# Top-k attention with a low-rank mixer: masking by a widened difference in the first two batches, and other rounding of the parameters

## The chip, the core and the metric

The kernel runs on one core of one Trainium2 chip. The metric is the device time of one execution in microseconds (us), the median over repeated runs. The core's engines work side by side, each through its own queue in program order: TensorE (PE, with its weight loads shown apart as PEld), VectorE (DVE), ScalarE (ACT), GpSimd (POOL) and SyncE (SP), which issues the transfers.

## What is computed

Eight batches, eight heads, 576 positions, head width 64. Attention keeps in each row of scores the 32 largest; its result is mixed along the sequence by two thin matrices of rank 32, and goes through a two-layer network with a residual.

```python
scores = scale * np.matmul(q, k.transpose(0, 1, 3, 2))
kth = np.partition(scores, -top_k, axis=-1)[..., -top_k:-top_k + 1]
mask = scores >= kth
scores = np.where(mask, scores, -1000000000.0)
scores = scores - np.max(scores, axis=-1, keepdims=True)
attn = np.exp(scores)
attn = attn / (np.sum(attn, axis=-1, keepdims=True) + 1e-09)
x = np.matmul(attn, v)                    # heads side by side: (batch, seq, 512)
h = x.transpose(0, 2, 1) @ U @ V          # rank 32
u = x + h.transpose(0, 2, 1)
out = u + np.maximum(u @ w_ch1, 0.0) @ w_ch2
```

The four parameters `U`, `V`, `w_ch1`, `w_ch2` arrive as 64-bit floating-point numbers. The engines have no such type, so the kernel takes the two 32-bit words of each number apart and joins them to a 32-bit number with integer and floating-point operations.

## The kernel before

**Steps.** Two heads form a pair `g`; a batch has four pairs, so `g` runs from 0 to 31. A pair has five blocks of query rows: `t` = 0 to 3 with 128 rows, in which the two heads are two chunks of scores side by side, and `t` = 4 with the last 64 rows of both heads, stacked into one chunk. A step is `n = 5 g + t`, and the loop over `n` (L561) writes out by hand in which order the parts of neighbouring steps go into the engines' queues. Batch 0 is `n` = 0 to 19; `ALONE` is 20.

**The parts of a step.** `scores(g, t)` multiplies on PE and lets ACT copy the scores to `Ssb`, which has three buffers. `front(g, t)` is a generator: each `yield` hands back to the loop, which decides when its next part is issued. It finds the 32nd largest score of each row on DVE in four rounds of "the eight largest" (`first` L317, then `m` L329) with three replacements between them (`rr` L325). Then it masks and weighs. Head 0 (chunk 0) was weighed early by ACT (`weigh`, the Exp of L297, right after `nmax` L321), and DVE masks its weights with L334, which also gives their sum. Head 1 is masked by POOL: L332 writes a large negative number where a score is under the threshold, L333 adds it to the scores, and ACT weighs after that, with the sum from the accumulator. The weights are `E`, with three buffers. `turns(g, t)` turns `E` on PE in pieces of four, four and one transposes (two pieces for `t` = 4), and ACT copies each piece to `PT`. `values(g, t)` multiplies `PT` by the values; ACT copies the product to `XT`, or for `t` = 4 scales it into `x` with the reciprocal of the sums `den` (L377 adds 1e-9, L378 inverts).

**Mixer and network.** `mixed(g, wait)` turns `XT` back, scales it on POOL (L419), multiplies by `U` (`pT`, `Tb`) and `V` and adds the residual (`up`), which gives `uT`, the input of the network. `mlp(b)` yields after every matmul: L462 for the first layer, whose result ACT passes through Relu to `hT` (L474), and L481 for the second. `fill()` takes from it a share of matmuls at fixed places of a step, so that batch b's network runs among the attention steps of batch b+1. In batch 0 there is no network to fill with.

**Parameters.** `next_params` moves 36 slabs through three stages: a load from memory (`f64_raw`), `f64_parts` with three ACT operations (L157, L159, L160) and a maximum on POOL (L158), and in the next call `f64_join` with a shift on DVE (L168) and two additions on POOL (L169, L171).

**The order in step n, up to ALONE.** First `first` of n; the rest of the turns of n-2; `scores` of n+1; `values` of n-2; `nmax` and the early Exp of n with its first round of replacements; `next_params`; the first piece of turns of n-1; the late Exp of n-1; the further rounds of n; its masks. After ALONE the same parts are spread between calls of `fill()`. PE, ACT, DVE and POOL keep the order in which the program issues.

Of the kernel before, what the change touches and what calls it, by code (L numbers as in the profile page):

```python
# [14 lines left out]
TOPK = 32  # L15
NEG = -3.0e38

TINY = 2.0**-15


@with_exitstack
def kernel(
# [80 lines left out]
    U = const.tile([P, NT + 1, R], F32, name="U")  # L103

    V = const.tile([NT * R, S], F32, name="V")

    step = const.tile([P, 1], F32, name="step")
    nc.vector.memset(step, 2.0**23)
    nudge = const.tile([P, 1], F32, name="nudge")
    nc.vector.memset(nudge, 0.4 * TINY)  # L110

    def rows(t):
        return P if t < NT else TAIL
# [27 lines left out]
    def f64_parts(raw, out):  # L141

        n, w = raw.shape[0], raw.shape[-1] // 2
        d = "p f" if len(raw.shape) == 3 else "p"
        low, hi = (raw.rearrange(f"{d} (w two) -> {d} w two", two=2)[..., i] for i in range(2))
        low8 = raw.bitcast(U8).rearrange(f"{d} (w eight) -> {d} w eight", eight=8)[..., 3]
        if out is None:
            if not spare:  # L150

                uT = mlpp.tile([P, NC, S], F32, tag="uT", name="uT")
                words = uT.rearrange("p c n -> p (c n)").bitcast(U32)
                spare.extend(words[:, i * SLAB : (i + 1) * SLAB] for i in range(NT))
            out = spare.pop()[0:n, 0:w]
        bits = out.bitcast(U32)
        nc.scalar.activation(bits.bitcast(F32), hi.bitcast(F32), AF.Abs)  # L157
        nc.gpsimd.tensor_scalar(bits.bitcast(F32), bits.bitcast(F32), TINY, None, ALU.max)  # L158
        nc.scalar.activation(low, low8, AF.Identity, bias=step[0:n], scale=(1 + 2.0**-10) / 32)  # L159
        nc.scalar.activation(hi.bitcast(F32), hi.bitcast(F32), AF.Sign, bias=nudge[0:n])  # L160
        return hi, bits, low

    def f64_join(hi, bits, low, outs):

        nc.vector.tensor_single_scalar(bits, bits, 3, ALU.logical_shift_left)  # L168
        nc.gpsimd.tensor_tensor(bits, bits, hi, ALU.add)  # L169
        for dst, form in outs:  # L170
            nc.gpsimd.tensor_tensor(dst.bitcast(U32), form(bits), form(low), ALU.add)  # L171
# [123 lines left out]
    def weigh(chunk, E, nmax, total=None):  # L295

        nc.scalar.activation(E, chunk, AF.Exp, bias=nmax, scale=SCALE, accum_out=total)  # L297

    def front(g, t):

        if t == 0:
            dens[g] = small.tile([P, 2 * NT + 1], F32, tag="den", name="den", bufs=3)
        chunks, den = S2s.pop((g, t)), dens[g]
        n = len(chunks)
        E2 = attn.tile([P, 2 * S], F32, tag="E", name="E", bufs=3)
        Es = [E2[:, c * S : (c + 1) * S] for c in range(n)]
        sums = [den[:, 2 * t + c : 2 * t + c + 1] for c in range(n)]
        probs[g, t] = E2  # L310
        curs, ms = list(chunks), [None] * n
        first = small.tile([P, 2, 8], F32, tag="first", name="first", bufs=3)
        nmax = small.tile([P, 2], F32, tag="nmax", name="nmax", bufs=4)
        order = (1, 0) if n == 2 else (0,)
        for c in order:
            ms[c] = first[:, c]
            nc.vector.max(ms[c], curs[c])  # L317
        yield
        for i in range(1, TOPK // 8):
            if i == 1:  # L320
                nc.scalar.mul(nmax[:, 0:n], first[:, 0:n, 0], -SCALE)  # L321
                weigh(chunks[0], Es[0], nmax[:, 0:1])
            for c in order:
                nxt = attn.tile([P, S], F32, tag="rr", name="rr", bufs=3)
                nc.vector.match_replace(nxt, ms[c], curs[c], NEG)  # L325
                curs[c] = nxt
            for c in order:
                ms[c] = small.tile([P, 8], F32, tag="m8", name="m8", bufs=8)
                nc.vector.max(ms[c], curs[c])  # L329
            yield  # L330
        if n == 2:
            nc.gpsimd.tensor_scalar(Es[1], chunks[1], ms[1][:, 7:8], NEG, ALU.is_lt, ALU.mult)  # L332
            nc.gpsimd.tensor_tensor(chunks[1], chunks[1], Es[1], ALU.add)  # L333
        nc.vector.scalar_tensor_tensor(  # L334
            out=Es[0],
            in0=chunks[0],
            scalar=ms[0][:, 7:8],
            in1=Es[0],
            op0=ALU.is_ge,
            op1=ALU.mult,  # L340
            accum_out=sums[0],
        )
        if t == NT:
            del qkTs[g]
        yield
        if n == 2:
            weigh(chunks[1], Es[1], nmax[:, 1:2], sums[1])
        yield

    def turns(g, t):  # L350
# [16 lines left out]
        nc.scalar.copy(PT[:, NT * nh], tp)  # L367
        yield

    def values(g, t):  # L370

        PT = PTs.pop((g, t))
# [1 line left out]
        O = ps_t.tile([P, P], F32, tag="tp", name="O")  # L374
        if t == NT:
            den, x = dens[g], xs[g % 2]
            nc.vector.tensor_scalar_add(den, den, 1e-9)  # L377
            nc.vector.reciprocal(den, den)  # L378
            for j in range(NT + 1):
                nc.tensor.matmul(  # L380
                    O,
# [23 lines left out]
    def mixed(g, wait):  # L405

        b, gi = divmod(g, NPAIR)
        if gi == 0:
            uTs[b] = mlpp.tile([P, NC, S], F32, tag="uT", name="uT")
        XT, den = XTs.pop(g), dens.pop(g)  # L410
        X = xs[g % 2]
        tp = ps_t.tile([P, NT, P], F32, tag="tp", name="tp")
        for t in range(NT):
# [141 lines left out]
    t = 0  # L555
# [5 lines left out]
    for n in range(STEPS + 2):  # L561
# [6 lines left out]
            fronts[n] = front(g, t)  # L568
            next(fronts[n])
        here, last = fronts.get(n, iter(())), fronts.pop(n - 1, iter(()))  # L570
        if n <= ALONE:
            next(turning, None)
            next(turning, None)
            if n < ALONE:
                scores(*divmod(n + 1, CH))
            fill()
            if n >= 1:
                turning = turns(*divmod(n - 1, CH))
            if n == ALONE:

                next(turning)
                next(turning)
            if n >= 2:
                values(*divmod(n - 2, CH))
            next(here)
            if n == ALONE:
                values(*divmod(n - 1, CH))
                mixing.append(mixed((n - 1) // CH, 1))
                fill()
                scores(*divmod(n + 1, CH))  # L590
                while mixing:
                    fill()
            next_params(1)
            if n and n < ALONE:
                next(turning)
            fill()
            next(last, None)
            next(ready, None)
            next(here)
            fill()  # L600
            if n >= 2 and (n - 2) % CH == NT:
                mixing.append(mixed((n - 2) // CH, 3))
            next(here)
            if n in (11, 16):
                next_params(1)
            next(here)
            fill()
            continue
        fill()
        next(turning, None)  # L610
        fill()
        next(turning, None)
        fill()
# [4 lines left out]
        if n + 1 < STEPS:  # L618
            scores(*divmod(n + 1, CH))
        next(here, None)  # L620
        next_params(1)
        if n - 2 >= ALONE and (n - 2) % CH == NT:
            mixing.append(mixed((n - 2) // CH, 4))
# [2 lines left out]
        fill()  # L626
        if n <= STEPS:
            turning = turns(*divmod(n - 1, CH))
        next(turning, None)
        fill()  # L630
        next(here, None)
        next(last, None)
# [37 lines left out]
```

## Time and profile before

| | us |
|---|---|
| median of 10 runs | 1872.44 |
| lowest and highest | 1869.05 and 1873.53 |
| the profiled execution | 1873.53 |
| its span, from the first instruction to the last | 1871.6 |
| PE busy in the span | 1754.3 (94%) |
| DVE busy | 1621.1 (87%) |
| ACT busy | 1009.5 (54%) |
| POOL busy | 689.3 (37%) |
| mean granted clock of PE | 0.963 |

The profile is one execution. In its strips the span is cut into 40 slices of some 47 us, with the busy share of each in tenths. In a timeline a row gives start, duration, engine, line, operation, what is written and read, how many instructions were merged, and in brackets how long the engine was idle before and what ended that. A row of stretches gives, for PE, PEld, DVE, ACT and POOL, the busy time in the stretch, then the granted clock of PE, the share of the transfer engines and the rate.

The groups that the change touches, from the profile's list of groups: L334 on DVE 160 times, 854 ns each, 136.7 us; L332 on POOL 128 times, 2242 ns, 287.0 us; L333 on POOL 128 times, 1409 ns, 180.3 us; L297 on ACT 288 times, 777 ns, 223.9 us.

### The profile page before, as it was taken

The page shows a single profiled execution, that of the slowest core. Times are in us where ns is not written, and L with a number is a line of the kernel's source. Part 1 is how long each engine was busy: PE and PEld are TensorE (multiplying, and loading weights), DVE is VectorE, ACT ScalarE, POOL GpSimd, SP SyncE. Part 2 cuts the span into 40 slices and gives each one's busy share as a digit, 9 for nine tenths or more (in the row PEclk, how much of TensorE's full clock was granted, in tenths as well). Part 3 has the DMA queues.
Part 4 walks back from the last instruction along what each step waited for, and adds up shares of the span by engine and source line. Part 5 has one row for each costly group of instructions (what it writes and reads, how often), then busy time and mean ns, then how long its engine had stood idle before and what let it go on. Part 6 is the DMA issues. An engine that isn't in the chain of part 4 may idle for free.

```text
span 1871.6 us, 29270 instructions
## 1 busy us (share of the span) xinstructions
PE 1754.3 (94%) x10528; PEld 1327.3 (71%) x10528; DVE 1621.1 (87%) x3312; ACT 1009.5 (54%) x2467; POOL 689.3 (37%) x470
## 2 busy tenths in 40 slices
PE   5565698999999999999999999999999999999999
PEld 3444466688677877788777877778777877778777
DVE  7999989899999999999999999999999999996000
ACT  4566676665555555555555556565655655554211
POOL 3667688533223332332323333323233232322000
PEclk7667799999999999999999999999999999999999
DMA  3222222100001010101001010010001010000000
GB/s 86 65 71 74 73 82 77 41 24 24 17 18 31 21 32 20 28 22 26 14 24 30 22 32 19 23 27 20 21 20 31 24 30 21 9 8 7 6 14 12
DMA packets 127296, 58.23 MB, mean 31 GB/s; under 512 B 89904, under 2 KB 124976, under 8 KB 127152
## 3 DMA queue, kind: packets, MB, share of 16 engines
q1 hardware_dynamic: 126096, 56.10, 11.2%
q8 instruction: 84, 1.38, 0.3%
q14 instruction: 60, 0.49, 0.1%
q10 hardware_dynamic: 1056, 0.26, 0.1%
HBM read 46.89 MB, written 9.44 MB: 30 GB/s over the span
## 4 chain that ended last, share of the span: by engine, by line
PE 82%; DVE 11%; ACT 3%; POOL 1%; issue 1%; DMA 0%; DVEq 0%; POOLq 0%; SPq 0%; ACTq 0%
PE mm L462 27%; PE mm L481 25%; PE sc L271 8%; PE O L393 6%; PE tp L361 6%; DVE rr L325 4%; DVE m L329 4%; PE up L437 2%; PE O L380 2%; DVE first L317 1%; PE O L390 1%; PE tp L251 1%; DVE E L334 1%; PE tp L509 1%; PE up L439 1%
## 5 line engine op out<-in xcount | busy, mean ns | idle before, releaser
L329 DVE MAX8 m<-rr 128x8 f32<-128x576 f32 x864 | 614.8, 749 | 5.3
L481 PE MATMUL mm<-hT,w 128*128 128x256 f32 (+1 forms) x2048 | 562.7, 410 | 0.0
L462 PE MATMUL mm<-uT,w 128*128 128x256 f32 (+1 forms) x2048 | 558.3, 411 | 1.5 <-ACT hT L474 1.5
L332 POOL TENSOR_SCALAR E<-Ssb,m 128x576 f32<-128x576 f32 x128 | 287.0, 2242 | 621.5 <-DVE m L329 498.2
L462 PEld LDWEIGHTS mm<-uT,w 128*128 128x128 f32 x2048 | 363.9, 190 | 108.5 <-issue 28.0
L481 PEld LDWEIGHTS mm<-hT,w 128*128 128x128 f32 x2048 | 360.8, 190 | 97.8 <-issue 22.7
L325 DVE MATCH_REPLACE8 rr<-m,rr 128x576 f32<-128x576 f32 x576 | 427.8, 743 | 0.0
L361 PE MATMUL tp<-ident,E 128*128 128x128 f32 x1152 | 186.1, 287 | 59.4 <-ACT E L297 42.6
L362 ACT COPY PT<-tp 128x512 f32<-128x512 f32 x288 | 168.2, 584 | 119.6 <-PE tp L361 117.8
L297 ACT ACTIVATE E<-Ssb,nmax 128x576 f32<-128x576 f32 x288 | 223.9, 777 | 6.9 <-POOL Ssb L333 1.7
L361 PEld LDWEIGHTS tp<-ident,E 128*128 128x128 f32 x1152 | 145.3, 147 | 112.8 <-ACT E L297 55.0
L271 PE MATMUL sc<-qkT 64*128 64x288 f32 (+1 forms) x1280 | 213.2, 455 | 0.0
L325 DVE MATCH_REPLACE8 rr<-first,Ssb 128x576 f32<-128x576 f32 x288 | 211.8, 742 | 0.0
L317 DVE MAX8 first<-Ssb 128x8 f32<-128x576 f32 x288 | 205.4, 750 | 0.9 <-ACT Ssb L292 0.9
L334 DVE SCALAR_TENSOR_TENSOR E<-Ssb,m,E 128x576 f32<-128x576 f32 x160 | 136.7, 854 | 63.1 <-ACT E L297 47.0
L333 POOL TENSOR_TENSOR Ssb<-Ssb,E 128x576 f32<-128x576 f32 x128 | 180.3, 1409 | 10.7
L474 ACT ACTIVATE hT<-mm 128x320 f32<-128x320 f32 (+1 forms) x256 | 104.4, 408 | 119.8 <-PE mm L462 119.0
L402 ACT COPY XT<-O 128x128 f32<-128x128 f32 x128 | 34.1, 267 | 214.4 <-PE O L393 214.4
L271 PEld LDWEIGHTS sc<-qkT 64*128 64x128 f32 (+1 forms) x1280 | 110.6, 188 | 52.0 <-issue 25.8
L393 PE MATMUL O<-PT,va 128*64 128x128 f32 x2048 | 146.5, 287 | 0.0
L494 DVE TENSOR_TENSOR oT<-uT,mm 128x320 f32<-128x320 f32 (+1 forms) x8 | 3.6, 454 | 146.6 <-PE mm L481 146.6
L393 PEld LDWEIGHTS O<-PT,va 128*64 128x64 f32 x2048 | 114.7, 142 | 16.6 <-issue 2.5
(75 smaller groups left out, 1545.7 us busy)
## 6 DMA issues: line engine op xcount, KB each, us to landing
raw<-in_moe_w_ch_dram SPq DMA_DIRECT2D x32, 512.0 KB, 3.7
va<-in_v_dram SPq DMA_DIRECT2D x64, 128.0 KB, 2.4
out_dram<-ob SPq DMA_DIRECT2D x64, 128.0 KB, 1.9
ld_q<-in_q_dram SPq DMA_DIRECT2D x63, 128.0 KB, 2.7
ld_k<-in_k_dram SPq DMA_DIRECT2D x63, 128.0 KB, 2.8
ld_ends<-in_q_dram SPq DMA_DIRECT2D x32, 32.0 KB, 2.2
ld_ends<-in_k_dram SPq DMA_DIRECT2D x32, 32.0 KB, 2.2
vd<-in_v_dram SPq DMA_DIRECT2D x64, 16.0 KB, 2.0
```

What stands on the lines that cost most here:

```text
L271: nc.tensor.matmul(sc[slice(0, n) if t < NT else half(h), h, 0:HALF], lhsT=qkT[half(h), 0, cols(t)], rhs=qkT[half(h), 1, i * HALF : (i + 1 ...
L297: nc.scalar.activation(E, chunk, AF.Exp, bias=nmax, scale=SCALE, accum_out=total)
L317: nc.vector.max(ms[c], curs[c])
L325: nc.vector.match_replace(nxt, ms[c], curs[c], NEG)
L329: nc.vector.max(ms[c], curs[c])
L332: nc.gpsimd.tensor_scalar(Es[1], chunks[1], ms[1][:, 7:8], NEG, ALU.is_lt, ALU.mult)
L333: nc.gpsimd.tensor_tensor(chunks[1], chunks[1], Es[1], ALU.add)
L361: nc.tensor.transpose(tp[:, j, :], E2[:, a : a + P], ident)
L362: nc.scalar.copy(PT[:, NT * h : NT * h + NT], tp)
L393: nc.tensor.matmul(O[half(h)], lhsT=va[:, h, j, :], rhs=PT[:, NT * h + j], start=False, stop=(j == NT - 1),)
L462: nc.tensor.matmul(ph[:, 0:w], lhsT=w1[:, cc, f * P : (f + 1) * P], rhs=uT[:, cc, lo:hi], start=(cc == 0), stop=(cc == NC - 1),)
L481: nc.tensor.matmul(po[:, 0:w], lhsT=w2[:, f, c * P : (c + 1) * P], rhs=hTs[f][:, 0:w], start=(f == 0), stop=(f == NF - 1),)
```

## The change

Three things are edited.

**Rounding.** `f64_parts` loses the POOL maximum. The upper word is scaled by 2^-112 in the first ACT operation (Copy with a scale in place of Abs), the lower part is formed with another bias and scale and written as a 32-bit float, and the third ACT operation stays, with a different small constant. `f64_join` is unchanged.

**First batch's last steps.** In steps 18 and 19 no chunk goes over POOL: all chunks are weighed early and masked by DVE. The order of steps 19 and 20 is written anew: in step 19 the turns of 17 and 18 and the values of 17 and 18 are issued, the first eight columns of `den` are inverted, and `mixed` begins, one step sooner; step 20 turns 19 and goes on. Step 19 has no `next_params`.

**Eased steps.** `eased(g, t)` is true in the first two batches but for steps 18 and 19. There neither head is weighed early, DVE masks nothing and POOL's L332 falls away. ACT forms `least`, the threshold times 2^96, and a Relu of 2^96 times (threshold minus score), which is zero for a score that is kept and huge for one that is not; POOL subtracts that from the scores; ACT weighs both heads with their sums. The addition of 1e-9 to `den` goes to ACT. This stands in two further parts of `front`, which the loop issues in the step after. The loop's order is changed to suit: up to step 18 all turns of n-2 are issued together and after `scores` of n+1, and in the second batch two pieces of turns are issued together. In batch 0 a further slab of parameters is taken in each step with t = 1 instead of in steps 11 and 16.

```diff
-        nc.scalar.activation(bits.bitcast(F32), hi.bitcast(F32), AF.Abs)
-        nc.gpsimd.tensor_scalar(bits.bitcast(F32), bits.bitcast(F32), TINY, None, ALU.max)
-        nc.scalar.activation(low, low8, AF.Identity, bias=step[0:n], scale=(1 + 2.0**-10) / 32)
+        nc.scalar.activation(bits.bitcast(F32), hi.bitcast(F32), AF.Copy, scale=RESCALE)
+        lows = low.bitcast(F32)
+        nc.scalar.activation(lows, low8, AF.Identity, bias=four[0:n], scale=-(1 + 2.0**-10) * 2.0**-26)
         nc.scalar.activation(hi.bitcast(F32), hi.bitcast(F32), AF.Sign, bias=nudge[0:n])
...
+    def eased(g, t):
+        return g < 2 * NPAIR and (g, t) not in ((NPAIR - 1, NT - 1), (NPAIR - 1, NT))
...
+        ease = eased(g, t)
+        pooled = n == 2 and not ease and (g, t) != (NPAIR - 1, NT - 1)
+        early = range(0 if ease else 1 if pooled else n)
...
-                weigh(chunks[0], Es[0], nmax[:, 0:1])
+                for c in early:
+                    weigh(chunks[c], Es[c], nmax[:, c : c + 1])
...
-        if n == 2:
+        if pooled:
             nc.gpsimd.tensor_scalar(Es[1], chunks[1], ms[1][:, 7:8], NEG, ALU.is_lt, ALU.mult)
             nc.gpsimd.tensor_tensor(chunks[1], chunks[1], Es[1], ALU.add)
-        nc.vector.scalar_tensor_tensor(
-            out=Es[0],
...
+        for c in early:
+            nc.vector.scalar_tensor_tensor(
+                out=Es[c],
...
         yield
-        if n == 2:
-            weigh(chunks[1], Es[1], nmax[:, 1:2], sums[1])
+        if ease:
+            least = small.tile([P, 2], F32, tag="least", name="least", bufs=3)
+            nc.scalar.mul(least[:, 0:n], final[:, 0:n, 7], WIDEN)
+            for c in order:
+                nc.scalar.activation(
+                    Es[c], chunks[c], AF.Relu, bias=least[:, c : c + 1], scale=-WIDEN
+                )
+                nc.gpsimd.tensor_tensor(chunks[c], chunks[c], Es[c], ALU.subtract)
+            yield
+        for c in order:
+            if c not in early:
+                weigh(chunks[c], Es[c], nmax[:, c : c + 1], sums[c])
+        if ease and t == NT:
+            nc.scalar.activation(den, den, AF.Identity, bias=eps)
         yield
...
+    def inverse(g, lo, hi):
+        den = dens[g][:, lo:hi]
+        if not eased(g, NT):
+            nc.vector.tensor_scalar_add(den, den, 1e-9)
+        nc.vector.reciprocal(den, den)
...
+        if n >= ALONE - 1 and n <= ALONE:
+            list(turning)
+            if n < ALONE:
+                scores(*divmod(n + 1, CH))
+            list(turns(*divmod(n - 1, CH)))
+            if n < ALONE:
+                values(*divmod(n - 2, CH))
+                next(here)
+            values(*divmod(n - 1, CH))
+            if n < ALONE:
+                inverse(g, 0, 2 * NT)
+                next(here)
+                mixing.append(mixed(g, 1))
+                fill()
+                next(here)
+                next(here)
+                continue
...
+        if n < ALONE:
+            scores(*divmod(n + 1, CH))
+            list(turning)
+            fill()
+            if n >= 2:
+                values(*divmod(n - 2, CH))
+            next(here)
+            next(last, None)
+            next_params(1)
+            fill()
+            next(ready, None)
+            next(here)
+            fill()
+            next(last, None)
+            if n >= 2 and (n - 2) % CH == NT:
+                mixing.append(mixed((n - 2) // CH, 3))
+            next(here)
+            if t == 1:
+                next_params(1)
+            next(here)
             fill()
             if n >= 1:
                 turning = turns(*divmod(n - 1, CH))
...
         next(turning, None)
+        if eased(*divmod(n - 2, CH)):
+            next(turning, None)
...
         next(here, None)
+        if eased(*divmod(n - 1, CH)):
+            next(last, None)
         next_params(1)
...
-        next(turning, None)
+        if not eased(*divmod(n - 1, CH)):
+            next(turning, None)
```

## The prediction

> **What bounds the kernel now.** I read the busy strips first, then busy time by stretches, then the timeline of single attention steps. A step n is one block of 128 query rows of one pair of heads (n = 5g + t; t = 4 is the short block); batch 0 is n = 0 to 19, batch 1 n = 20 to 39.
>
> ```profile
> PE   5565698999999999999999999999999999999999
> DVE  7999989899999999999999999999999999996000
> ACT  4566676665555555555555556565655655554211
> PEclk7667799999999999999999999999999999999999
> ```
>
> Until about 235 us DVE is full and PE is not; from 350 us on PE is full to the end. Whatever is won must be won before that: an earlier start of the first MLP matmul (L462, at 237.20), or less PE idling in batch 1.
>
> ```profile
> 150.00:200.00 50.00, 31.74 (x185) 21.73 (x183) 49.09 (x101) 33.93 (x75) 36.20 (x24) 0.73 0.27 79
> 250.00:300.00 50.00, 45.34 (x267) 31.18 (x268) 47.49 (x96) 37.71 (x86) 40.81 (x26) 1.00 0.25 77
> 300.00:350.00 50.00, 43.23 (x257) 30.02 (x256) 44.60 (x96) 33.71 (x76) 42.39 (x29) 0.97 0.20 59
> 400.00:450.00 50.00, 50.00 (x332) 40.79 (x332) 48.75 (x101) 28.58 (x72) 16.98 (x11) 1.00 0.09 22
> ```
>
> Columns: stretch, length, then PE, PEld, DVE, ACT, POOL busy, and the granted clock. PE idles 4.7 + 6.8 us in 250:350, and 2.9 us more in 450:500: some 14 us in all. After 500 us it hardly idles until the end.
>
> ```profile
> 31.48 2.22 POOL L332 TENSOR_SCALAR E<-Ssb,m 128x576 f32<-128x576 f32 x1 [3.84 <-DVE m L329]
> 32.15 0.82 DVE L334 SCALAR_TENSOR_TENSOR E<-Ssb,m,E 128x576 f32<-128x576 f32 x1
> 32.90 1.42 DVE L317 MAX8 first<-Ssb 128x8 f32<-128x576 f32 x2
> 33.78 1.40 POOL L333 TENSOR_TENSOR Ssb<-Ssb,E 128x576 f32<-128x576 f32 x1
> 37.57 0.77 ACT L297 ACTIVATE E<-Ssb,nmax 128x576 f32<-128x576 f32 x1
> 38.49 1.11 PE L361 MATMUL tp<-ident,E 128*128 128x128 f32 x4 [4.36 <-ACT E L297]
> ```
>
> One step: DVE masks head 0 (L334), POOL masks head 1 (L332, L333), ACT weighs it (L297), PE turns it. DVE goes straight on to the next step and waits for nobody. A full step takes DVE 10.98 us here and 11.21 once each carries a 512-wide shift L168; from 11.08 to 224.14 batch 0 takes 213.1 us, 53.3 a pair.
>
> **What DVE and POOL lose.** L334 costs DVE 0.82 a step. Batch 0 has 20 of them before and 3 after (two in step 18, one in 19): 17 x 0.82 = 13.9 us. Three additions L377 (1.03 us where they meet POOL) go to ACT: 3.1. Waits behind POOL of L334 and L168 (up to 1.53 and 1.29 us instead of 0.82 and 0.41) shrink by some 2. DVE alone would need 19 us less, 48.2 a pair. POOL loses L158 (1.49 each, 31 times) and 3.63 a step, and gains two subtractions of 1.41: it was some 70% busy and gets lighter, and nobody is held by it. The max was only waited for by L168 (8.1 us in all, in batch 1, where DVE isn't last). The three ACT operations per parameter slab keep their shapes: nothing. Batch 0 fetches an extra slab in each t = 1 (four, not two, and none in step 19): the same transfers on SP, two of them some 60 us earlier, and their ACT time is in the laps. The divided `inverse` of g = 3 adds two DVE operations of 0.15 and 0.22 us, in cover of the handover's PE work. Relu (L474) and Exp already alternate with a single table load of 1.28 us, so the new Relu costs no further one.
>
> The shift now stands 4.1 us after the step's first MAX8, and by the durations below the first subtraction ends about then. If it meets one, the row for that is L168 at 208.95, 1.29 against 0.41 us. The Trainium skill (SBUF — State Buffer, Who interferes with whom) says that such a pair blocks for the whole instruction, which speaks against two subtractions in a row; L377 at 74.23, ending 0.03 us after POOL's L333, agrees. By the page it would be up to 1.41 us a shift, by the row 0.9; I put 0 to 18 us on DVE in batch 0, and take it as hidden, because DVE is no longer last there:
>
> **What ACT gains, and the new loop.** Per full step ACT gets `least` (0.24 us from start to start, as L321 at 13.26), two Relus (0.68, as Exp at 56.06 to 56.74) and one more accumulator read (0.09): 1.7 us. That fits into ACT's share. What doesn't is the order: before, E of head 0 came from DVE; now all of E(n-1) is the end of ACT's queue in step n, and PE's turns of it, ACT's copies PT, values, and the copy XT stand in ACT's queue ahead of the next `nmax`, `least`, Relus and Exps. That is a closed loop, one turn a step:
>
> - E ready to XT: 8 transposes and the ninth behind the first PT copy, last PT copy at 2.7 us, then values. Cold (L390 at 51.70 to XT at 54.44) these take 2.8, warm 1.6: XT at 4.4 to 5.6.
> - XT to the next E: XT 0.16, nmax 0.24, least 0.24, Relus 1.36, three slab operations 0.56 + 0.64 + 0.64, qkT 0.46, Exps 1.54: 5.8 (start to start, mostly from the row of ACT operations between 219.77 and 223.84).
>
> A full lap is 10.2 to 11.4 us, against 10.4 that DVE then needs; the short step doesn't shorten it, where DVE needs 6.0.
>
> ```profile
> 160.18 1.11 PE L361 MATMUL tp<-ident,E 128*128 128x128 f32 x4 [3.67 <-ACT E L297]
> 161.44 2.25 PE L271 MATMUL sc<-qkT 64*128 64x288 f32 x8
> 163.62 0.49 PE L390 MATMUL O<-PT,vd 128*128 128x128 f32 x2
> 164.04 1.09 PE L393 MATMUL O<-PT,va 128*64 128x128 f32 x16
> ```
>
> After an idle gap PE runs at half clock for about 3.4 us (four transposes 1.11, later 0.66), so I take the colder half. The Trainium skill (TensorE: Matmul & The Clock Gate, What's actually happening) gives a free-running window of about 3.4 us; by it the values would be half warm, XT at about 5.0.
>
> The five laps of a pair: t = 0 (one Relu and Exp fewer, no qkT) 9.2; t = 1 (short turns, two `x`) 10.4; t = 2 (starts behind the extra slab of t = 1, 1.84, and `x` 0.5) 12.5; t = 3 (uT copies, short-step score copies) 12.0; t = 4 10.7. Sum 54.8, ends 51.0 (warm) and 56.6 (cold): no better than 53.3. E(0) is ready at 27.0 (DVE begins step 1 at 21.1, and nmax to Exp take 5.9); steps 2 to 4, which carry small slabs, 32.4; two pairs 109.6; the last four laps 45.8 (with 1.36 of early weighing): E(17) at 214.7, ends 202 and 222.
>
> **The handover.** Before, 13.1 us pass from the last L334 (ends 224.14) to L462. After, from E(17): turns 17 (2.4), scores (1.2 to 2.3), turns 18, two values, XT, Exp and mask of 19 (the mask alone 0.82), turns 19 (0.9), values 19 (1.5), x (0.6), pT, Tb, scores, up: 15 to 20, I take 17.2. First MLP matmul at 231.9 instead of 237.2: -5, ends -20 and +4.
>
> **Batch 1.** The same loop now has PE's MLP share in it. After the scores of n+1, PE has 5 to 8 MLP matmuls of 0.56 us (four in 2.32 at 291.10), mostly 7, 3.9 us, before it comes to the turns of E(n-1). ACT needs: last score copies 0.7, nmax and least 0.54, Relus 1.36, slab 1.88, hT 0.32, Exps 1.55: 6.35.
>
> ```profile
> 288.58 0.64 ACT L290 COPY Ssb<-sc 128x576 f32<-128x576 f32 x1 [0.42 <-PE sc L271]
> 289.69 0.23 ACT L321 ACTIVATE nmax<-first 128x2 f32<-128x2 f32 x1
> 290.64 0.67 ACT L157 ACTIVATE w<-raw 128x512 f32<-128x512 f32 x1
> 291.10 2.32 PE L462 MATMUL mm<-uT,w 128*128 128x320 f32 x8
> 291.86 0.77 ACT L160 ACTIVATE raw<-raw,nudge 128x512 f32<-128x512 f32 x1
> ```
>
> PE stands 2.4 us in such a step; 3.2 in a short one (5 matmuls), about 1 in t = 0. For n = 22 to 29, with slabs, 19 in all, and 2 more where the ninth transpose waits for PT copies behind a second slab. Without slabs (30 to 39) 0.5 a full step, 1.4 a short one: 6. Together 27 against the 14 idled before: +12; ends -14 (all covered) and +25 (1.2 more at each of 20 steps, where hT or POOL come late).
>
> **Sum.** The profiled execution took 1873.53 us (span 1871.6), 1.1 above the median. 1873.5 - 5 + 12 = 1880.5, on the median's scale 1880. Later batches keep their work and PE's 99.6%: 0.
>
> **Rivals.**
> - Faster: the loop is hidden. PE stays warm, laps cost DVE's 48.2, so 19 us come off batch 0, and 4.6 off the handover (13.1 to 8.5, PE being caught up); with batch 1 unchanged 1850, with its 14 us gone too 1836. With laps at the warm end (-20, and batch 1 at half its loss, +6) 1859. For it: DVE is the full engine in both batches, and of PE's stalls between 237 and 345 us 6.4 are turns of E that wait for ACT already, and cost little. Against: ACT's order, in which XT stands ahead of nmax. It decides if a full lap stays under 10.4 us.
> - A draw: laps at 52.5 a pair (-11), batch 1 +9: 1871, within 3.7 us.
> - The port: DVE keeps the lead but pays 18 us of blocked shifts in batch 0: 1850 + 18 = 1868. Against: the first subtraction ends at about the shift's start.
>
> **Chances.** Slower by the loop 0.50, alone 1876 to 1898; the hidden loop and the port, faster, 0.34; a draw 0.16. About 0.2%, 3.7 us, is what can be told from no change. Range 1846 to 1898: the full gain (1836) and the worst loss stay outside, about 0.15.
>
> **What would show it.** Right: in batch 0 DVE busy falls from 49 to about 44 in 50 us, its idle put down to ACT (slab copies for L175, score copies); first MLP matmul near 232; in 250:350 PE idles over 20 us, put down to ACT's E. Wrong: DVE at 49 in 50 with full steps of 10.4 us, the MLP starting before 220, PE full from 240 on.

## The result, and the profile after

The changed kernel takes 1921.81 us (median of 8 runs, 1920.16 to 1923.08) against 1872.23 (29 runs of the kernel before): ratio 1.0268, 95% interval 1.0259 to 1.0277. It is slower by 49.6 us where 8 were forecast, and outside the range (1846 to 1898).

The strips of the changed kernel's page, read as those of before:

```profile
PE   4667688888899999999999999999999999999999
DVE  7988897777799999999999999999999999997000
PEclk7666798999999999999999999999999999999999
```

DVE is no longer full in most of the slices 3 to 11 (batches 0 and 1), and PE is full only from slice 12 on, some 530 us. The same stretches as before:

```profile
150.00:200.00 50.00, 31.65 (x159) 21.66 (x159) 40.93 (x84) 37.28 (x88) 25.77 (x20) 0.67 0.21 61
250.00:300.00 50.00, 39.85 (x205) 26.52 (x203) 42.91 (x84) 39.31 (x90) 26.92 (x20) 0.91 0.23 66
300.00:350.00 50.00, 42.52 (x237) 29.74 (x236) 36.57 (x72) 32.48 (x76) 19.66 (x16) 0.92 0.23 70
400.00:450.00 50.00, 43.67 (x268) 34.02 (x262) 34.59 (x70) 31.92 (x84) 10.77 (x9) 0.97 0.09 21
```

In 150:200 DVE falls from 49.1 to 40.9 of 50 us. In 250:350 PE idles 10.2 + 7.5 us instead of 4.7 + 6.8, at 0.91 and 0.92 of its clock; in 400:450, where it had been full, it idles 6.3. ACT, which got the work, is busy less than 40 us of 50 in all four.

One lap of the loop in batch 0, rows picked from the timeline of the changed kernel:

```profile
118.74 0.76 ACT L304 ACTIVATE E<-Ssb,nmax 128x576 f32<-128x576 f32 x1
119.65 1.97 PE L396 MATMUL tp<-ident,E 128*128 128x128 f32 x8 [3.19 <-ACT E L304]
122.13 0.27 ACT L402 COPY PT<-tp 128x128 f32<-128x128 f32 x1
123.18 1.98 PE L433 MATMUL O<-PT,va 128*64 128x128 f32 x16
125.21 0.27 ACT L442 COPY XT<-O 128x128 f32<-128x128 f32 x1 [2.80 <-PE O L433]
125.70 0.78 ACT L373 ACTIVATE E<-Ssb,least 128x576 f32<-128x576 f32 x1
128.23 0.76 ACT L304 ACTIVATE E<-Ssb,nmax 128x576 f32<-128x576 f32 x1
```

PE has waited 3.19 us for the Exp (L304). It turns E, ACT copies, PE multiplies with the values, and ACT stands 2.80 us until it can copy XT. Only behind XT come the next Relu (L373) and Exp. Each engine waits for the other once a lap.

Two divisions of the 49.1 us between the profiled spans (1920.7 and 1871.6) are of use. By the first matmul of the network (L502, before L462): it comes at 242.50 instead of 237.20, +5.3; from there to the end it takes 1678.2 instead of 1634.4, +43.8. By steps, from one `nmax` to another: step 20 begins 11.5 later, steps 20 to 29 take 132.6 instead of 118.5 (+14.1), steps 30 to 39 126.2 instead of 100.7 (+25.5), and the rest 2.0 less. The stretch of steps 30 to 39, where no slabs are left, before and after:

```profile
348.61:449.30 100.69, 100.69 (x657) 80.24 (x656) 98.23 (x201) 58.73 (x150) 34.35 (x23) 1.00 0.10 25
```

```profile
374.22:500.40 126.18, 108.46 (x657) 83.22 (x656) 90.59 (x182) 73.91 (x190) 30.12 (x24) 0.96 0.08 20
```

PE idles 17.7 us where it idled none, and is busy 7.8 us longer with the same 657 matmuls. The clock was lower in three pieces of this stretch, and full in the rest:

```profile
390.26:393.67 3.41, 3.41 (x11) 2.39 (x10) 3.38 (x8) 0.27 (x1) 0.00 (x0) 0.50 0.20 53
431.22:434.63 3.41, 3.41 (x11) 2.59 (x10) 3.38 (x8) 1.00 (x3) 0.00 (x0) 0.50 0.00 0
492.66:496.07 3.41, 3.41 (x11) 2.67 (x10) 3.38 (x8) 1.17 (x3) 0.13 (x1) 0.50 0.00 0
```

Three times 3.41 us at half clock cost at most 5.1 us, so not all of the 7.8 is the clock. The two largest of PE's waits in the stretch (us in total, times, longest):

```profile
PE tp L396 <- ACT E L304: 12.7, 7, 2.9
PE pT L465 <- POOL x L459: 3.6, 2, 2.2
```

### The profile page after: what moved, and what is told of

Read it like the earlier page. It is cut to its first block, busy times and chain, and to the rows that moved or that the text cites. A ratio compares the mean times of both kernels' runs of the same rounds, so it can differ in the third digit from the quotient of the medians.

```text
span 1920.7 us, 29161 instructions
## 1 busy us (share of the span) xinstructions
PE 1776.0 (92%) x10528; PEld 1338.9 (70%) x10528; DVE 1593.9 (83%) x3234; ACT 1064.5 (55%) x2618; POOL 615.4 (32%) x439
## 4 chain that ended last, share of the span: by engine, by line
PE 73%; issue 1%; POOL 1%; ACT 0%; POOLq 0%; DVE 0%; DVEq 0%; ACTq 0%
PE mm L502 23%; PE mm L521 23%; PE sc L278 7%; PE O L433 5%; PE tp L396 5%; PE O L420 1%; PE up L477 1%; PE O L430 1%; PE tp L258 1%; PE tp L549 1%; PE up L479 1%; PE tp L454 1%; PE pT L465 1%; PE tp L401 1%; POOL oT L537 0%
## 5 line engine op out<-in xcount | busy, mean ns | idle before, releaser
L502 PE MATMUL mm<-uT,w 128*128 128x256 f32 (+1 forms) x2048 | 561.7, 413 | 4.8 <-ACT hT L514 4.8
L502 PEld LDWEIGHTS mm<-uT,w 128*128 128x128 f32 x2048 | 367.1, 192 | 114.2 <-issue 29.6
L351 DVE MAX8 m<-rr 128x8 f32<-128x576 f32 x576 | 409.8, 748 | 2.2
L354 POOL TENSOR_SCALAR E<-Ssb,final 128x576 f32<-128x576 f32 x96 | 215.7, 2247 | 542.2 <-DVE final L351 417.8
L332 DVE MAX8 first<-Ssb 128x8 f32<-128x576 f32 x288 | 205.2, 749 | 44.8 <-ACT Ssb L299 41.0
L304 ACT ACTIVATE E<-Ssb,nmax 128x576 f32<-128x576 f32 x288 | 223.1, 775 | 17.9 <-POOL Ssb L376 13.9
L351 DVE MAX8 final<-rr 128x8 f32<-128x576 f32 x288 | 204.9, 749 | 2.7
L376 POOL TENSOR_TENSOR Ssb<-Ssb,E 128x576 f32<-128x576 f32 x69 | 97.4, 1431 | 270.4 <-ACT E L373 206.2
L357 DVE SCALAR_TENSOR_TENSOR E<-Ssb,final,E 128x576 f32<-128x576 f32 x123 | 105.0, 854 | 69.7 <-ACT E L304 53.6
L355 POOL TENSOR_TENSOR Ssb<-Ssb,E 128x576 f32<-128x576 f32 x96 | 135.3, 1409 | 8.0
```

The source lines that it names most:

```text
L502: nc.tensor.matmul(ph[:, 0:w], lhsT=w1[:, cc, f * P : (f + 1) * P], rhs=uT[:, cc, lo:hi], start=(cc == 0), stop=(cc == NC - 1),)
```

## Experiments

The theory: ACT's order closes a loop with PE, and one lap bounds a step. The rivals: ACT's added work costs as such; another part of the change costs; PE's clock is the cost. "First" is the first matmul of the network in the profiled execution.

| run | median, us | ratio to before (95%) | first, us |
|---|---|---|---|
| no_ease | 1865.62 | 0.9963 (0.9948 to 0.9977) | 233.77 |
| ease_batch0 | 1874.78 | 1.0011 (1.0001 to 1.0020) | 242.59 |
| ease_batch1 | 1912.42 | 1.0217 (1.0202 to 1.0233) | 232.82 |
| loop_opened | 1845.82 | 0.9857 (0.9843 to 0.9872) | 213.75 |
| act_load | 1882.41 | 1.0066 (1.0051 to 1.0081) | 241.42 |
| relus_twice | 1981.25 | 1.0595 (1.0579 to 1.0611) | 262.18 |
| relus_twice_opened | 1874.30 | 1.0020 (1.0010 to 1.0029) | 220.45 |
| slab_behind | 1940.19 | 1.0366 (1.0349 to 1.0384) | 260.96 |
| no_subtraction | 1903.17 | 1.0169 (1.0155 to 1.0183) | 242.15 |
| warm_fill | 1917.88 | 1.0254 (1.0237 to 1.0271) | 242.00 |
| warm_batch0 | 1926.56 | 1.0295 (1.0281 to 1.0309) | 246.37 |
| opened_batch0 | 1844.33 | 0.9855 (0.9841 to 0.9870) | 212.46 |

**Which part.** Three kernels differ from the changed one in the line that says which steps are eased:

```diff
-        return g < 2 * NPAIR and (g, t) not in ((NPAIR - 1, NT - 1), (NPAIR - 1, NT))
+        return False                                  # no_ease
+        return g < NPAIR and (g, t) not in ...        # ease_batch0
+        return NPAIR <= g < 2 * NPAIR                 # ease_batch1
```

> No eased step at all: what is left is the rounding without POOL's maximum, the two last steps of batch 0 weighed early, and the new order. Loop theory: first MLP matmul at 230 to 236 us (the handover 4 to 7 us shorter), the stretch after it 1630 to 1640, total 1864 to 1872 us. Rival (rounding or order to blame): above 1890 us.

> The changed kernel with eased steps in batch 0 alone (batch 1 masked as before, by DVE and POOL). Loop theory: batch 1 lost 43.8 us after the first MLP matmul (1678.2 us against 1634.4), because PE waits for E at the end of ACT's queue once a step and falls to a lower clock; without it the stretch from the first MLP matmul to the end is again 1632 to 1640 us, and the total 1874 to 1884 us. Rival (the cause lies in the rounding, or in the new order of steps 19 and 20): the total stays above 1905 us.

> Eased steps in batch 1 alone; batch 0 masked by DVE and POOL as before, in the changed order. Loop theory: first MLP matmul at 230 to 238 us (DVE at its 53 us a pair, a shorter handover), the stretch after it as long as in the changed kernel, 1670 to 1682 us; total 1902 to 1918 us. Rival (batch 0's state, for instance slabs that come late, causes batch 1's loss): the stretch is under 1650 us.

In all three the total and the first matmul came in as expected; the stretches behind it (1629.6, 1630.9 and 1682.5 us) lie within 1.1 us of the ranges given. What stays without easing (the rounding, whose third ACT operation keeps the constant that it had, the two last steps, and the new order of the loop) gains 7.0 us (1872.65 for the kernel before in these runs); no run takes these apart. On top of that, easing costs 9.2 in batch 0 and 46.8 in batch 1. Their sum, 56.0, is the 56.2 between the changed kernel and no_ease: the whole loss is in the eased steps, five sixths of it in batch 1.

**Order or load.** In loop_opened the same instructions stand in another order: the Relus of step n-1 at the head of step n, its Exps ahead of the values of n-2, and the like in batch 1.

```diff
         if n < ALONE:
+            next(last, None)
             scores(*divmod(n + 1, CH))
             list(turning)
-            fill()
-            if n >= 2:
-                values(*divmod(n - 2, CH))
             next(here)
-            next(last, None)
             next_params(1)
             fill()
+            next(last, None)
+            if n >= 2:
+                values(*divmod(n - 2, CH))
...
-            next(last, None)
...
+        if eased(*divmod(n - 1, CH)):
+            next(last, None)
         fill()
         next(turning, None)
...
         next(turning, None)
         fill()
+        if eased(*divmod(n - 1, CH)):
+            next(last, None)
...
-        if eased(*divmod(n - 1, CH)):
-            next(last, None)
```

> All of the change, but in both batches the Relus of step n-1 are issued at the head of step n and its Exps before the values of n-2, so that no ACT operation between one E and the next waits for PE's values. The same instructions. Loop theory: the loop is open; in batch 0 DVE is last again, with full steps of 10.4 us, the first MLP matmul at 212 to 225 us, in batch 1 PE idles under 15 us; total 1835 to 1862 us. Rival (ACT's added work, or POOL's subtractions holding the shared port, is what costs): the same instructions cost the same, 1905 us or more.

It takes 1845.82: 76.0 us less than the changed kernel by order alone, and less than before. As expected, the first matmul of the network comes at 213.75, and PE idles 12.2 us from there to 500 us. Its stretches:

```profile
150.00:200.00 50.00, 34.50 (x189) 24.31 (x189) 49.41 (x102) 42.20 (x100) 28.61 (x22) 0.70 0.29 82
300.00:350.00 50.00, 47.25 (x287) 34.08 (x286) 41.10 (x85) 34.87 (x90) 20.42 (x17) 0.97 0.12 29
```

DVE is full again in batch 0 (49.41), and ACT does more in 50 us (42.20) than in the changed kernel (37.28), so it had time to spare there. PE works 47.25 us in 300:350. Before it can copy XT, ACT waits for PE's values; in batch 0 (40 to 210 us) this wait all but goes away, first the changed kernel, then loop_opened (us in total, times, longest):

```profile
ACT XT L442 <- PE O L433: 29.8, 12, 2.8
```

```profile
ACT XT L442 <- PE O L433: 1.7, 2, 1.4
```

In a step of its timeline the values stand behind the Exps, and what ACT waits for is now mostly DVE (`least`, 15.9 us in the same stretch):

```profile
116.12 0.21 ACT L371 ACTIVATE least<-final 128x2 f32<-128x2 f32 x1 [2.13 <-DVE final L351]
116.36 1.44 ACT L373 ACTIVATE E<-Ssb,least 128x576 f32<-128x576 f32 x2
122.18 0.78 ACT L304 ACTIVATE E<-Ssb,nmax 128x576 f32<-128x576 f32 x1
122.94 0.64 ACT L428 ACTIVATE x<-O,den 64x64 f32<-64x64 f32 x2
```

The load alone was put into the kernel before, behind the late Exp, on scores that nothing reads any more:

```diff
+        if g < 2 * NPAIR:
+            nc.scalar.mul(extra, nmax[:, 0:1], 2.0)
+            for chunk in chunks:
+                nc.scalar.activation(chunk, chunk, AF.Relu, bias=extra, scale=-1.0)
```

> The kernel before, with the ACT work of the change added to it at the end of ACT's queue of each step of batches 0 and 1, to no purpose (a small product and one Relu for each chunk, over scores that are no longer needed), and nothing taken from DVE or POOL. Loop theory: E of head 0 still comes from DVE, so there is no loop, and ACT has room: 1870 to 1882 us. Rival (ACT's load): above 1900 us.

It costs 11.8 us (1870.62 for the kernel before in these runs), 0.4 above the upper edge: load is a cost, but a small part of what easing costs. The other test doubles the Relus, once in the changed kernel's order and once in the opened one:

```diff
             for c in order:
+                nc.scalar.activation(
+                    Es[c], chunks[c], AF.Relu, bias=least[:, c : c + 1], scale=-WIDEN
+                )
+            for c in order:
                 nc.scalar.activation(
                     Es[c], chunks[c], AF.Relu, bias=least[:, c : c + 1], scale=-WIDEN
                 )
```

> The changed kernel with every Relu of the eased steps issued twice, the first set to no purpose: 1.36 us more on ACT in a full step, 0.68 in a short one, 46 us over the 38 eased steps; ACT is 55% busy in the changed kernel. Loop theory: the two stand in the loop, so nearly all of it is paid, and PE gets colder besides: 1955 to 1985 us against 1921.8. Rival (ACT has room, and POOL's subtractions or DVE set the step): 1922 to 1930 us.

> The kernel with the opened loop (1845.8 us), with the same Relus issued twice, the same 46 us more on ACT. Loop theory: ACT's queue in a step grows from about 8.1 to 9.5 us and stays under DVE's 10.4 in full steps; only short steps show it: 1846 to 1862 us. Rival (it is ACT's load and not the order that costs): 1880 us or more.

In the closed loop the second Relus cost 59.4 us, as expected. In the opened one they cost 28.5, neither the 0 to 16 expected nor the rival's 34 or more: a miss. In the profiled executions 6.7 us of it lie ahead of the first matmul of the network, 20.7 behind it. For the first part ACT's row says why:

```profile
100.00:150.00 50.00, 34.94 (x192) 23.73 (x192) 49.30 (x104) 47.38 (x109) 29.33 (x23) 0.71 0.29 82
```

With 47.38 of 50 us ACT had no room left in batch 0: 42 to 44 us of 50 were taken without the second Relus. In batch 1 that doesn't explain it. ACT has room there, and PE works 43.56 us where it worked 47.25:

```profile
300.00:350.00 50.00, 43.56 (x246) 31.43 (x247) 35.45 (x74) 38.23 (x89) 22.55 (x19) 0.93 0.13 36
```

The opened order issues the Relus of batch 1 at the head of a step, ahead of turns whose PT copies ACT then makes later, and PE's wait for these copies is longer, first without, then with the second Relus (from the first matmul of the network to 505 and 530 us):

```profile
PE tp L401 <- ACT PT L397: 8.4, 5, 3.1
```

```profile
PE tp L405 <- ACT PT L401: 18.4, 9, 5.3
```

That is 10 of the 20.7 us; the rest isn't put down to a cause. So the opened order takes the changed kernel's loop away, but PE still waits for ACT's queue, and added work is paid there though ACT has room.

**What stands in the lap.** slab_behind moves the slab's ACT operations from ahead of the Exps to behind them. The expectation speaks of batch 1; the edit did the same in the eased steps of batch 0.

```diff
             next(here)
             next(last, None)
-            next_params(1)
             fill()
...
             next(last, None)
+            next_params(1)
...
-        if eased(*divmod(n - 1, CH)):
+        ease = eased(*divmod(n - 1, CH))
+        if ease:
             next(last, None)
-        next_params(1)
+        else:
+            next_params(1)
...
         next(last, None)
+        if ease:
+            next_params(1)
```

> The changed kernel with the parameter slab's operations of each eased step of batch 1 (1.9 us of ACT) moved behind the Exps instead of ahead of them, all else as it is. By the theory of the lap, ACT's queue order inside the lap sets PE's stand: of about 1.9 us a step in some 10 steps that carry slabs, most comes back: 1900 to 1912, first MLP matmul unchanged near 242.5. Rival, that batch 1 loses through ACT's load or through PE's clock and not by what stands ahead of the Exps: 1917 to 1926.

Neither came: 1940.19. The first matmul of the network comes 18.5 us later, and from there the time is the same (1677.5 against 1678.2). The waits in batch 0 show the reason, first for the changed kernel, then for slab_behind (us in total, times, longest):

```profile
ACT E L304 <- POOL Ssb L376: 0.9, 2, 0.5
```

```profile
ACT E L304 <- POOL Ssb L376: 19.4, 33, 1.5
```

An Exp can't start before POOL has subtracted (1.4 us behind the Relu). The slab's operations had filled that wait. Behind the Exps they hold up the PT copies instead, so the lap keeps the slab and gains the wait. In the slab steps of batch 1, where 1.9 us a step were expected back, the same is seen: the Exps wait 9.2 us for POOL (1.3 before the edit), and PE 8.9 us for PT copies (0.9). That points at the steps without slabs, 30 to 39; there the changed kernel's waits say

```profile
ACT E L304 <- POOL Ssb L376: 10.3, 16, 1.3
```

and no_subtraction leaves POOL's subtraction out in these ten steps, so it doesn't mask there:

```diff
-                nc.gpsimd.tensor_tensor(chunks[c], chunks[c], Es[c], ALU.subtract)
+                if g < 6:
+                    nc.gpsimd.tensor_tensor(chunks[c], chunks[c], Es[c], ALU.subtract)
```

> The changed kernel without POOL's subtraction in the steps n = 30 to 39, so that the scores there are weighed unmasked; all other instructions and their order are kept. In the changed kernel's trace ACT's Exps wait 10.3 us for that subtraction between 374 and 500 us, and TensorE idles 17.7 us in the same ten steps, where the prediction had 6. If the wait stands in the lap: TensorE idles 7 to 11 us there, the lower clock gives back a part of its 7.8 us as well, and the whole takes 1906 to 1914, with the first MLP matmul unchanged near 242.5 and the steps 20 to 29 still 130 to 135 us long. Rival, that ACT's own instructions and TensorE's share of the network fix the lap and the wait lies in their cover: 1917 to 1923.

1903.17, a little under the lower end. Steps 20 to 29 take 132.5 as before the edit; steps 30 to 39:

```profile
373.85:483.62 109.77, 103.18 (x658) 79.98 (x656) 90.60 (x182) 72.08 (x191) 7.30 (x8) 1.00 0.09 23
```

PE idles 6.6 us there instead of 17.7: 4.4 for E instead of 12.7, and 0.6 instead of 3.6 for `x`, which POOL scales for the mixer. The clock is full throughout, and the matmuls take 103.2 us instead of 108.5. The difference, 5.3, fits the three pieces at half clock. Against the 100.7 of the kernel before 2.5 us remain that stand at full clock too; no run says what they are.

**The clock.** warm_fill gives PE two more matmuls of 512 columns at the end of each eased step of batch 1; warm_batch0 gives it twelve of 128 columns in each step 4 to 17 ahead of the turns. Both write to a buffer that nothing reads.

```diff
+        if eased(*divmod(n - 1, CH)):                 # warm_fill, end of a step
+            idle = ps_t.tile([P, NT, P], F32, tag="tp", name="idle")
+            for _ in range(2):
+                nc.tensor.matmul(idle.rearrange("p t n -> p (t n)"), lhsT=ident, rhs=w1[:, 0, 0:MAIN], ...)
...
             scores(*divmod(n + 1, CH))
+            if n >= 4:                                # warm_batch0
+                idle = ps_m.tile([P, C], F32, tag="mm", name="idle")
+                for _ in range(12):
+                    nc.tensor.matmul(idle[:, 0:P], lhsT=ident, rhs=ident, start=True, stop=True)
```

> The changed kernel with two matmuls of 512 columns to no purpose at the end of each step of batch 1, where PE waits for E: some 1.8 us of PE work in a wait of 1 to 3. Theory that part of batch 1's loss is the lower clock (0.91 to 0.93 granted between 250 and 400 us, 1.00 before the change): the clock there rises to 0.97 or more, and the time falls by 4 to 12 us, to 1910 to 1918. Rival (the clock follows from the waits but costs nothing of its own, since PE waits anyway): the same or slower, 1920 to 1940 us.

> The changed kernel with twelve more matmuls of 128 columns (identity by identity, into a buffer that batch 0 doesn't use) on TensorE in each step from n = 4 to 17, between the scores of n+1 and the turns of n-1, where TensorE waits for ACT's E. They change no data. By the prediction's split of the lap, E ready to XT takes 4.4 us warm and 5.6 us cold: if the clock in the lap is a cost of its own, the granted clock in 50 to 200 us rises from about 0.65 to 0.85 or more and 0.5 to 1.2 us a lap over 14 laps comes back, first MLP matmul at 225 to 236 instead of 242.5, and the whole at 1904 to 1915. Rival, that ACT's own operations and POOL's subtraction fill the lap whatever TensorE does: first MLP matmul at 240 to 244, 1918 to 1925. Later than 245 would say that the added matmuls are themselves in the way.

warm_fill's stretches 250:300 and 350:400:

```profile
250.00:300.00 50.00, 43.49 (x223) 27.74 (x221) 42.13 (x85) 39.44 (x90) 26.96 (x20) 1.00 0.23 69
350.00:400.00 50.00, 45.59 (x258) 30.86 (x257) 36.27 (x74) 29.87 (x76) 19.97 (x17) 1.00 0.11 28
```

The granted clock is 1.00 in both (0.91 and 0.93 in the changed kernel). The median is 3.9 us lower, within the range expected, but the two intervals, 1.0237 to 1.0271 and 1.0259 to 1.0277, overlap: the clock's recovery is shown, a gain of time is not. What a warm clock would be worth alone stays open, since the added matmuls take time themselves, two of them 1.88 us, and stand partly in PE's waits.

warm_batch0 is a miss: 4.8 us slower, the first matmul at 246.37, though the granted clock rose from 0.64, 0.67 and 0.67 in the three stretches from 50 to 200 us to 0.81, 0.91 and 0.91. Two laps show two things. Where the added matmuls ended before E was ready, a lap went from 10.9 us (XT at 172.28 and 183.20) to 9.4 (177.22 and 186.64), and E ready to XT from 5.7 to 4.2. Where E came early, behind the scores of a short step, they stood in its way: the lap that begins with XT at 89.7 took 16.5 us instead of 13.5, since E was ready at 95.5 and PE turned it from 102.2 on. The first, 1.5 us, is the clock's price in that lap (granted 1.00 instead of 0.50); the second hid it in the sum.

**The best version.** opened_batch0 has loop_opened's order in batch 0 and no easing in batch 1:

```diff
-        return g < 2 * NPAIR and (g, t) not in ((NPAIR - 1, NT - 1), (NPAIR - 1, NT))
+        return g < NPAIR and (g, t) not in ((NPAIR - 1, NT - 1), (NPAIR - 1, NT))
```

> The opened order of batch 0 (the eased Relus of step n-1 at the head of step n, its Exps before the values of n-2), with batch 1 not eased. If easing is worth something in batch 0 alone, and batch 1's share of the gain was only the undoing of batch 1's own loop: first MLP matmul near 214 as in the opened loop of both batches, from there 1630 to 1636 as with nothing eased in batch 1, so 1843 to 1850, like the opened loop of both (1845.8). Rival, that easing batch 1 gains as well once its loop is open: 1853 to 1862, slower than the opened loop of both by 7 or more. Slower than 1865.6 would say that the opened order itself is not what brought the gain in batch 0.

1844.33, as loop_opened: easing in the opened order pays 21.3 us in batch 0 (1865.62 for no_ease; the first matmul moves by 21.3 as well), and nothing in batch 1. No run has the opened order without easing, so a part of the 21.3 could be the order's own. It is 1.45% faster than the kernel before.

## Why the prediction was right in direction and wrong in size

**Right: the mechanism.** "That is a closed loop, one turn a step" is what loop_opened shows by order alone, and the place where the prediction looked for it (XT ahead of `nmax` in ACT's queue) is the place that the opened order undoes. Of the three signs named, DVE's is there from 100 us on (40.9 in 50, further down than the 44 named; 49.5 still in 50:100), with its idle put down to ACT: of the waits between 100 and 200 us 10.0 for `den`, whose addition had moved to ACT, and 6.3 for slabs. PE's idle in 250:350 is 17.6, not over 20, and 8.8 of it are put down to E, 4.8 to POOL's `x` and 3.8 to `hT`. The network's start went the other way: 242.5, later than before, where 231.9 was to be earlier. So the direction of the whole was right, and the sign of its first term wrong.

**Right: what DVE would need.** 48.2 us a pair were worked out. In loop_opened, where DVE is last, a pair takes 48.35 (MAX8 of one step to that of five steps later, 105.77 to 154.12). The port rival fell with it: of the 15 shifts between 60 and 205 us two take 1.44 us and two 0.59 where 0.41 is usual, some 2.5 us of excess and not 18. One reading behind the 19 us was off: the L334 of 1.53 us stands at 234.87, in batch 1; in batch 0 none is longer than 1.08.

**Wrong by 10.6 us: the laps of batch 0.** From E ready to E ready, us, in the steps 10 to 14 of the changed kernel (the last Exp's start plus 0.76 is E ready):

| lap in the step with | predicted | measured |
|---|---|---|
| t = 0 | 9.2 | 9.5 (119.50 to 128.99) |
| t = 1 | 10.4 | 11.0 (to 139.96) |
| t = 2 | 12.5 | 13.5 (to 153.50) |
| t = 3 | 12.0 | 13.1 (to 166.57) |
| t = 4 | 10.7 | 10.9 (to 177.49) |
| pair | 54.8, ends 51.0 and 56.6 | 58.0, beyond the cold end |

"XT to the next E" was right: 5.2 to 5.8 in the laps t = 2 to 4, 5.8 predicted. "E ready to XT" was put in the middle of 4.4 and 5.6 (10.7 - 5.8 = 4.9 in the lap t = 4, though the text says "the colder half"); measured 5.7 in plain laps, the cold end, and 7.7 in the laps t = 2 and 3, where a slab and then the score copies (1.1 us, not in the sum) stand ahead of the PT copies, or the mixer's and the short step's matmuls ahead of the turns. The prediction let the half clock last "about 3.4 us" after a gap. In the lap t = 4 and the next it lasted 20.48 us without a break, with PE busy 15.72 of them:

```profile
164.98:185.46 20.48, 15.72 (x74) 10.54 (x74) 14.12 (x27) 14.21 (x36) 9.49 (x8) 0.50 0.17 54
```

So E(17) is ready at 226.0, not 214.7. The handover was right (16.5 us, 17.2 predicted), and the first matmul comes at 242.5 where 231.9 was given, 1.3 beyond the worse end.

**Wrong by 32 us: batch 1.** The sum had 27 us of idle PE against 14, at full clock: +12, at worst +25, where +43.8 was measured behind the first matmul. (The worst end doesn't follow from its own words: 1.2 us more at each of 20 steps is 24 on top of +12, some +36. The measured +43.8 lies beyond that too.) For the steps with slabs the idle term holds: 21 predicted for 22 to 29, 24.3 measured in 20 to 29 (12.7 before). The step that failed is "Without slabs (30 to 39) 0.5 a full step, 1.4 a short one: 6": 17.7. Its working took the slab's 1.88 us out of ACT's row and put the Exp's wait for POOL, whose subtraction the slab had covered, at nothing; POOL coming late stands only in the worse end, and of POOL it says "nobody is held by it":

```profile
402.61 1.44 ACT L373 ACTIVATE E<-Ssb,least 128x576 f32<-128x576 f32 x2
403.46 2.78 POOL L376 TENSOR_TENSOR Ssb<-Ssb,E 128x576 f32<-128x576 f32 x2 [2.96 <-ACT E L373]
404.91 0.78 ACT L304 ACTIVATE E<-Ssb,nmax 128x576 f32<-128x576 f32 x1 [0.59 <-POOL Ssb L376]
406.27 0.78 ACT L304 ACTIVATE E<-Ssb,nmax 128x576 f32<-128x576 f32 x1 [0.50 <-POOL Ssb L376]
407.20 0.98 PE L396 MATMUL tp<-ident,E 128*128 128x128 f32 x7 [1.59 <-ACT E L304]
```

This is step 32 of the changed kernel: 0.59 and 0.50 us of ACT's waiting, and PE's 1.59 behind them. PE also waits for POOL's `x`, 3.6 us in these ten steps. Without the subtraction PE idles 6.6 us in them, close to the 6 that were predicted.

The second part was missing altogether: the longer busy time. PE is busy 7.8 us longer in steps 30 to 39, with the same matmuls, and 2.4 longer in 20 to 29, though that stretch holds 578 of them instead of 611. The sum took PE's clock as full in batch 1, although the loop was said to make PE stand in every step; of the 7.8, some 5 go with the three pieces at half clock, and 2.5 stay open. So the 39.6 us by which these twenty steps grew are 29.3 of idle (24.3 + 17.7 - 12.7) and 10.2 of busy time.

**The forecast's middle** came from two opposed terms, -5 and +12. Both were on the kind side, and for one reason: the lap was summed from the operations that the trace of before shows, and what those operations would newly wait for (the copies behind a slab, POOL behind a Relu, a cold PE) was put at nothing or at the middle end.

## What to carry to other kernels

When work is moved to an engine with room, draw the queue order of that engine and of the one that it feeds: if an output of the second stands ahead of the next input to it, they are in a loop, and the lap, not the busy share, is the price. Sum the lap with every wait that a neighbour used to hide, at the cold clock; then try the same instructions in another order, because here that was worth 76 us against the 12 of the added work. And judge an edit by stages: the same easing with the opened order pays 21 us where DVE is last and nothing where PE is.

## What was not expected of the hardware

- Gaps in PE's work of less than 3 us cost twice. In steps 30 to 39 of the changed kernel each of the three pieces at half clock, 3.41 us long, begins 0.5 to 1.3 us after PE ended a gap: the gaps of 2.24, 2.49 and 2.92 us (the first a wait for POOL's `x`, the others for E). The gaps of 2.13 us and less drew none, and in no_subtraction, where the longest is 1.31 us, the clock is full. In the 3.41 us ahead of the three pieces PE was busy 1.17, 1.28 and 0.89 us, so it need not stand throughout. The Trainium skill (TensorE: Matmul & The Clock Gate, Why this matters for your kernels) advises against idle gaps of more than about 3 us; here shorter ones had a price, and by that rule these steps would have lost no clock.
- Two more matmuls in each eased step of batch 1 cost no time (1917.88 and 1921.81, intervals overlapping). The clock that they kept up may have paid for them, or the waits in which they partly stand; no run tells the two apart.
- The Trainium skill (Perfetto Trace Analysis, Optimizing Scalar/DVE Operations) says that work may be moved to ScalarE when VectorE is saturated. Both outcomes are here: with the opened order it gains 21.3 us in batch 0, and with the changed kernel's order the same work, on an ACT that is 55% busy, loses 56.2.
- POOL's subtractions hardly got in the way of DVE's shifts: L175 has a median of 0.42 us over 18 shifts of 512 columns in the opened loop's batch 0, and up to 1.46 in single cases.
